# A replanned order of steps for a fused sigmoid-attention and token-mixing kernel on one core

## The chip, the cores and the metric

The kernel runs on one core of one Trainium2 chip. A core has five engines that run their own instruction queues side by side: TensorE (PE, matrix products and transposes into PSUM banks; PEld is its weight load), VectorE (DVE), ScalarE (ACT), GpSimd (POOL) and SyncE (SP, which here issues most DMAs). The metric is the device time of one execution in microseconds (us), lower is better. The runs before the change took 180.97, 180.97 and 181.77 us, a median of 180.97.

## The reference

For 8 batches, 12 heads, 448 rows and a head size of 64, in float32:

```python
scores = scale * np.matmul(q, k.transpose(0, 1, 3, 2)) - np.log(S)
attn = 1.0 / (1.0 + np.exp(-scores))
x = attn @ v                      # heads side by side: (8, 448, 768)
W_tok = scale * np.einsum('bsd,btd->bst', x @ w_q, x @ w_k)
mixed = np.einsum('bst,btd->bsd', W_tok, x)
out = np.maximum(mixed, 0.0) @ w_out
```

A sigmoid replaces the softmax, so no row sums are needed. The kernel never forms `W_tok`: it multiplies `(x w_k)^T x` first (a 64 x 768 matrix per batch), then mixes with `x w_q`.

## The kernel before

**Units of work.** The 96 head-batches go in 24 quads of four heads: quad n is heads 4j to 4j+3 of batch u, n = 3u + j. A quad's 448 rows are cut into 7 blocks of 64. For each quad there are these steps; the letters are those of the order string `PLAN`, which is written out in full and read by one loop at the end:

- Loads (SP queue, L177 and L188) bring q, k and v of a quad in float32 into one of eight buffers of 448 KB. `ORDER` is the order of loads and casts.
- Casts to bf16: most on POOL (L201 and L224 for q and k, L218 for v, 128 x 896 each). A `.` ahead of a name in `ORDER` puts that cast on VectorE, a capital letter on ScalarE, and a `*` drops both load and cast and issues one casting DMA from POOL's queue straight into the bf16 buffer (L213).
- Transposing q and k, in one of three forms. Form `c` with `d`: POOL swaps 32-row blocks with six copies (L163, L166, L169, two each, function `arrange`), then VectorE makes two stream transposes of 128 x 448 (L285); `c` needs the copies of L166 and `d` those of L169. Form `r` with `s` and `z`: no POOL copies, but VectorE makes two transposes of 128 x 448 (L278) and four of 32 x 448 (L254). Form `q` with `k` (and `a` with `b`): TensorE transposes, VectorE copies the result out (L316, L302).
- `S`, 168 times: TensorE makes one block's scores for four heads (L328, four matmuls of 64 x 448) into two banks, ScalarE applies the sigmoid (L333, 128 x 896).
- `P` (also `p`, `R`), 168 times: TensorE accumulates attention times v (L350); after the seventh block VectorE casts the result `xt` out (L359).
- `x`, `X`: TensorE transposes `xt` (L388, L372), VectorE copies `xn` (L401, L377). `W`, `w`, `L`, `l`: x times w_q and w_k (L425, L413); at the end of a tiled pass one half is copied (`wpart`, L420) and VectorE adds the other half (L421). `N`, `U`, `T`, `M`: the small products of the mixing (L440, L454, L469, L493, L507), the relu at L480 or L478.
- `O`, `o`, `Q` (also `I`, `i`): a part of the output product (L539, L579, L620); after the last part VectorE or ScalarE copies `o` out (L550, L552, L584, L653; the letter says which engine) and a DMA stores it.

**What sets the order.** Every engine takes its instructions strictly in the order in which the loop records them; there is no scheduler. Eight PSUM banks are handed out by the list `BANKS`, one entry per step that needs one. A cast is recorded on POOL as soon as its load is recorded and its target is free: the bf16 buffer `qk16` exists twice, so the q and k casts of quad n come after the transposes of quad n-2; `v16` exists four times.

Of the kernel before, what the change touches and what calls it, by code (L numbers as in the profile page):

```python
# [932 lines left out]
```

## Time and profile before

| | before |
|---|---|
| time, median of three runs | 180.97 us (180.97 to 181.77) |
| span of the profiled execution | 180.1 us |
| TensorE busy | 169.6 us, 94% |
| ScalarE busy | 159.0 us, 88% |
| VectorE busy | 145.6 us, 81% |
| GpSimd busy | 121.4 us, 67% |
| bytes moved by DMA | 47.31 MB |

The page gives the span of the profiled execution, from its first to its last instruction; its own time is not listed apart from the three runs. The 0.87 us between span and median lie outside the instructions.

How to read it: a busy share is a mean over stages. GpSimd's 67%, for example, hides that it does almost nothing in the last fifth of the span. In a timeline row the first number is the start in us from the span's start, the second the length, then engine, line, operation, output and input with their shapes, and in brackets what the engine sat idle for just before. TensorE rows overlap in their ends, so its pace is read from starts.

### The profile page before, as it was taken

The numbers are of one execution on the slowest core, as the hardware profiler recorded it, in microseconds if no ns is written. First come the engines' busy times: TensorE is split into PE (matmuls) and PEld (weight loads), VectorE is DVE, ScalarE is ACT, GpSimd is POOL, SyncE is SP. The second block draws the span as 40 slices with busy tenths as digits, with TensorE's granted clock in tenths as the row PEclk, the third lists the DMA queues.
The fourth block names the chain that finished last, engine by engine and source line by source line (L and its number), as shares of the span: only waits on it lengthen the run. The fifth ranks groups of instructions, "written<-read, shape, count | busy, mean of one in ns | idle before, by whom it ended". The sixth has DMA issues, their size and how long they took to land.

```text
span 180.1 us, 7907 instructions
## 1 busy us (share of the span) xinstructions
PE 169.6 (94%) x3440; PEld 112.2 (62%) x3440; DVE 145.6 (81%) x227; ACT 159.0 (88%) x208; POOL 121.4 (67%) x166
## 2 busy tenths in 40 slices
PE   7698899889899999999999999999999999999990
PEld 3334445444575555445667786678887788888660
DVE  3578899997989896889999999979898886768351
ACT  4699999999899999999999999999999989976300
POOL 1028799689999999999999999979979910010000
PEclk9999999999999999999999999999999999999999
DMA  5999999999999998899998889987795523505876
GB/s 177 355 372 349 322 383 381 280 302 356 342 294 349 339 265 267 217 319 365 343 300 315 217 288 305 342 322 213 200 338 173 135 64 73 137 4 122 201 208 175
DMA packets 27475, 47.31 MB, mean 263 GB/s; under 512 B 3888, under 2 KB 23600, under 8 KB 27440
## 3 DMA queue, kind: packets, MB, share of 16 engines
q1 hardware_dynamic: 26160, 44.64, 78.0%
q0 software_dynamic: 800, 1.18, 3.6%
q10 hardware_dynamic: 480, 0.98, 1.5%
q8 instruction: 27, 0.44, 1.0%
q14 instruction: 8, 0.07, 0.1%
HBM read 35.78 MB, written 11.01 MB: 260 GB/s over the span
## 4 chain that ended last, share of the span: by engine, by line
PE 56%; POOL 16%; DMA 15%; DVE 5%; ACT 2%; issue 2%; SPq 1%; POOLq 0%
PE banks L539 15%; PE banks L350 10%; PE banks L328 10%; PE banks L620 8%; DMA q<-in_q_dram 6%; POOL qk L201 5%; DMA w<-in_moe_w_k_dram 4%; DMA k<-in_k_dram 3%; POOL qk L169 3%; DMA wout<-wout 2%; ACT at L333 2%; POOL v L218 2%; PE banks L579 2%; PE banks L413 2%; POOL swap L163 2%
## 5 line engine op out<-in xcount | busy, mean ns | idle before, releaser
L333 ACT ACTIVATE at<-banks 128x896 bf16<-128x896 f32 x168 | 140.0, 948 | 3.4 <-PE banks L328 3.0
L328 PE MATMUL banks<-qk 64*64 64x448 bf16 x672 | 62.2, 358 | 3.3 <-ACT at L333 1.6
L350 PE MATMUL banks<-at,v 64*64 64x448 bf16 x672 | 47.3, 351 | 0.8 <-ACT at L333 0.7
L328 PEld LDWEIGHTS <-qk 64*64 64x64 bf16 x672 | 25.9, 105 | 20.7 <-issue 13.2
L539 PE MATMUL banks<-wout,mx 64*64 64x384 bf16 x672 | 36.6, 323 | 0.0
L201 POOL CAST qk<-k 128x896 bf16<-128x896 f32 x19 | 22.8, 1199 | 10.6 <-DVE qk L302 9.7
L350 PEld LDWEIGHTS <-v 64*64 64x64 bf16 x672 | 23.2, 107 | 8.6 <-issue 1.7
L539 PEld LDWEIGHTS <-mx 64*64 64x64 bf16 x672 | 23.3, 107 | 4.5 <-issue 0.5
L359 DVE CAST xt<-banks 128x896 bf16<-128x896 f32 x22 | 23.8, 1083 | 2.3 <-PE banks L350 1.8
L620 PE MATMUL banks<-wout,mx 128*128 128x384 bf16 (+1 forms) x138 | 24.4, 320 | 0.0
L480 DVE TENSOR_SCALAR mx<-banks 128x1024 bf16<-128x1024 f32 (+3 forms) x22 | 21.3, 972 | 1.9 <-PE banks L493 0.7
L201 POOL CAST qk<-q 128x896 bf16<-128x896 f32 x17 | 20.4, 1198 | 2.6 <-DMA q<-in_q_dram 1.3
L218 POOL CAST v<-v 128x896 bf16<-128x896 f32 x22 | 20.6, 950 | 1.4 <-DMA v<-in_v_dram 0.4
L620 PEld LDWEIGHTS <-mx 128*128 128x128 bf16 x138 | 12.3, 98 | 9.8 <-issue 3.2
L285 DVE STREAM_TRANSPOSE qk<-qk 128x448 f32<-128x448 f32 x28 | 17.0, 627 | 0.4 <-POOL qk L166 0.3
L163 POOL COPY swap<-qk 32x448 uint32<-32x448 uint32 x28 | 15.5, 554 | 2.3 <-DVE qk L201 0.7
L166 POOL COPY qk<-qk 32x448 uint32<-32x448 uint32 x28 | 15.8, 566 | 1.6
L169 POOL COPY qk<-swap 32x448 uint32<-32x448 uint32 x28 | 15.8, 564 | 1.6
L254 DVE STREAM_TRANSPOSE qk<-qk 32x448 f32<-32x448 f32 x24 | 15.3, 636 | 0.6
L422 POOL COPY wq<-wqk 64x448 bf16<-64x448 bf16 x3 | 1.7, 555 | 15.7 <-DVE wqk L421 15.7
L653 DVE COPY o<-banks 128x384 f32<-128x384 f32 x12 | 6.6, 553 | 5.7 <-PE banks L620 5.3
L653 ACT COPY o<-banks 128x384 f32<-128x384 f32 x9 | 4.4, 490 | 7.1 <-PE banks L620 6.9
(91 smaller groups left out, 206.5 us busy)
## 6 DMA issues: line engine op xcount, KB each, us to landing
q<-in_q_dram SPq DMA_DIRECT2D x24, 448.0 KB, 6.6
v<-in_v_dram SPq DMA_DIRECT2D x24, 448.0 KB, 6.3
k<-in_k_dram SPq DMA_DIRECT2D x23, 448.0 KB, 7.0
out_dram<-o SPq DMA_DIRECT2D x50, 192.0 KB, 3.9
wout<-in_moe_w_out_dram POOLq DMA_DIRECT2D x2, 576.0 KB, 12.2
wout<-wout SPq DMA_DIRECT2D x12, 96.0 KB, 6.2
out_dram<-o ACTq DMA_DIRECT2D x4, 192.0 KB, 3.5
k<-in_k_dram SPq DMA_DIRECT2D x1, 256.0 KB, 5.6
```

The lines of the kernel that those rows point to most:

```text
L163: eng.tensor_copy(out=z[lo], in_=w[hi, 0])
L169: eng.tensor_copy(out=w[lo, 1], in_=z[lo])
L201: COPY[e](out=f[:, :, "qk".index(nm)].rearrange("p e i d y -> p e y i d"), in_=ld.pop((nm, n)),)
L218: COPY[e](out=t16.rearrange("p b i d -> p (b i d)"), in_=ld.pop((nm, n)).rearrange("p b x -> p (b x)"),)
L285: nc.vector.transpose(out=qk[n][:, t].rearrange("p t i n -> p (t i n)").bitcast(F32), in_=w)
L328: nc.tensor.matmul(sc[HALF[h], g, 0:S], qk[n][HALF[g], h, 1, i, :], qk[n][HALF[g], h, 0].rearrange("p i n -> p (i n)"), start=True, stop=True,
L333: inst = nc.scalar.activation(at, sc[:, :, 0:S], ACTF.Sigmoid, bias=attn_bias, scale=attn_scale)
L350: nc.tensor.matmul(ps[HALF[g], h, 0:S], ld["v16", n][HALF[h], g, i, :], ats[n, i][HALF[h], g, :], start=(i == 0), stop=(i == NI - 1),)
L359: read(fb, COPY[eng](out=xt(u, j)[:, :, 0:S], in_=ps[:, :, 0:S]))
L480: inst = nc.vector.tensor_scalar(dst, ps, moe_scale, 0.0, ALU.mult, ALU.max)
L539: nc.tensor.matmul(ps[HALF[x], y, 0:NB], mx[HALF[y], u, b, 64 * (i - 3 * y) : 64 * (i - 3 * y) + 64], wout16[HALF[y], slot(y, b), x * NB : ...
L620: nc.tensor.matmul(ps, mxs[w][:, 2 * S * c + m * P : 2 * S * c + (m + 1) * P], wout16[:, c, w0:w1], start=(c == 0), stop=(c == NC - 1),)
```

## The change

The change replaces the tables that set the order and the way buffers are given out. What is computed is the same.

- `PLAN` and `BANKS` are written anew as one table: each step carries its bank. 168 `S`, 168 `P`-type and the other product steps remain in number, with some exceptions: six filler matmuls `F` and four fillers `f` at the start are gone, one `X` became an `x`, one `U` a `T` and one quad less is transposed on TensorE. In the changed program TensorE changes 59 times between whole and quartered use of its array once it has started.
- The transposing forms of quads 0 to 23 were `aarqrrqcrccccrccccrccccc` and are `aarrrrqcrccccrcccccccccc`: quad 3 goes from TensorE (`q`) to VectorE (`r`), and quad 18 from VectorE alone (`r`) to POOL copies with VectorE (`c`).
- Casts: q1, k1, q2, q12, q22, k22 and v22 were on VectorE and v19 on ScalarE. Now only k2 is on VectorE, and v6 and v23 come by casting DMAs; all others are on POOL.
- Output copies: ScalarE makes fewer of them before the last sigmoid, VectorE more.
- Tile pools become fixed buffers used in turn; a load takes any free one of the eight load buffers.

```diff
     PLAN = (
-        "ffSSSffKSSF11aSb1SFFrSFSFSSFSqSPPsPPSPzkPSPSPPPSxSrSsPPPPSPPS"
...
+        "S67 S23 K01 S67 S45 S23 a01 S45 b S67 1 S23 S45 S23 P01 S67 p p S23 r R S45 s p P S67 z "
...
     ORDER = (
-        ".q1 .k1 k2 .q2 q3 v0 w2 k3 v1 k4 q4 v2 w0 k5 q5 w1 v3 W5 v4 q6 k6 w4 k7 v5 q7 v6 q8 k8 k9 "
-        "q9 v7 q10 v8 k10 v9 k11 q11 k12 k13 v10 .q12 q13 v11 v12 v13 q14 k14 k15 q15 v14 q16 k16 "
-        "v15 q17 k17 k18 q18 q19 v16 v17 v18 k19 V19 W3 q20 .q22 q21 k20 W6 k21 .k22 v20 q23 k23 "
-        "v21 .v22 v23 "
+        "q1 k1 q2 .k2 v0 v1 q3 w2 k3 q4 k4 W5 v2 w0 v3 k5 q5 v4 w1 W3 q6 v5 k6 W6 q7 w4 *v6 k7 k8 "
+        "q8 q9 k9 v7 k10 v8 q10 v9 q11 k11 v10 k12 q12 k13 v11 q13 k14 v12 v13 q14 k15 q15 v14 "
+        "q16 k16 k17 q17 v15 v16 v17 q18 k18 v18 k19 q19 v19 k20 q20 q21 v20 k21 q22 k22 v21 v22 "
+        "k23 *v23 q23 "
...
+    lds = [singles.tile([P, 2 * RUN + PAD], F32, name=f"ld{n}") for n in range(8)]
+    v16s = [singles.tile([P, 2, NI, HD], BF16, name=f"v16{n}") for n in range(4)]
+    qks = [singles.tile([P, 2, 2, NI, NP], BF16, name=f"qk{n}") for n in range(8)]
+    qk16s = [singles.tile([P, 2, 2, NI, 32, 2], BF16, name=f"qk16{n}") for n in range(2)]
...
+    def turn(nm, bufs):
+        turns[nm] = turns.get(nm, -1) + 1
+        return bufs[turns[nm] % len(bufs)]
+
+    def borrow(key):
+        held[key] = free.pop(0)
+        return held[key]
...
-                pq[n] = p_c16.tile([P, 2, 2, NI, 32, 2], BF16, tag="qk16", name="qk16")
+                pq[n] = turn("qk16", qk16s)
...
-            if len(ring) >= 8 and ring[-8] not in cast:
+            if not free:
                 break
...
+        if (nm, n) in held:
+            free.append(held.pop((nm, n)))
         pump_loads()
```

The tables show where steps went only in the instruction order. Three places matter here. In these rows the changed program's lines stand about twelve higher: its L213 is L201 of before, L230 is L218, L175, L178 and L181 are L163, L166 and L169, L297 is L285, L371 is L359, L432 and L433 are L420 and L421. `ld` is a load buffer, `qk16` the cast q and k, `v16` the cast v, `swap` a scratch tile; numbers behind a name tell buffers apart.

POOL, the last quads. Before, from the k cast of quad 21 (its q was cast earlier) to the casts of v21 and v23; quad 22's casts are on VectorE, so only its copies stand here:

```order
L201 CAST qk16_2870<-k32_2619 128x2x2x224
L163 COPY swap_2881<-qk16_2870 32x448 x2
L166 COPY qk16_2870<-qk16_2870 32x448 x2
L169 COPY qk16_2870<-swap_2881 32x448 x2
L422 COPY wq21_120<-wqk1_118 64x448
L218 CAST v16_3060<-v32_2782 128x896
L163 COPY swap_3280<-qk16_3207 32x448 x2
...
L201 CAST qk16_3433<-q32_3056 128x2x2x224
L201 CAST qk16_3433<-k32_3058 128x2x2x224
L163 COPY swap_3436<-qk16_3433 32x448 x2
...
L218 CAST v16_3443<-v32_3209 128x896
L218 CAST v16_3624<-v32_3235 128x896
```

The same piece of POOL's order in the changed program, from quad 22's casts to quad 23's last copy:

```order
L213 CAST qk161_121<-ld1_101 128x2x2x224
L213 CAST qk161_121<-ld2_102 128x2x2x224
L175 COPY swap_3010<-qk161_121 32x448 x2
...
L230 CAST v161_109<-ld3_103 128x896
L230 CAST v162_110<-ld4_104 128x896
L213 CAST qk160_120<-ld6_106 128x2x2x224
L225 DMA v163_111<-in_v_dram 128x2x448
L213 CAST qk160_120<-ld7_107 128x2x2x224
L175 COPY swap_3235<-qk160_120 32x448 x2
L178 COPY qk160_120<-qk160_120 32x448 x2
L181 COPY qk160_120<-swap_3235 32x448 x2
```

Quad 22's two casts came to POOL, v21 and v22 now stand ahead of quad 23's casts and copies instead of behind them, and the casting DMA of v23 stands between quad 23's two casts.

VectorE, quad 7's two transposes (`qk16_781` before, `qk7` from `qk160` in the changed program), before:

```order
L285 STREAM_TRANSPOSE qk_977<-qk16_781 128x448
L401 COPY xn_950<-banks_88 128x2x4x128
L285 STREAM_TRANSPOSE qk_977<-qk16_781 128x448
L359 CAST xt5_116<-banks_88 128x2x448
L278 STREAM_TRANSPOSE qk_1086<-qk16_923 128x448 x2
```

And now:

```order
L413 COPY xn1_127<-banks_67 128x2x4x128
L371 CAST xt5_95<-banks_67 128x2x448
L297 STREAM_TRANSPOSE qk7_119<-qk160_120 128x448 x2
L290 STREAM_TRANSPOSE qk0_112<-qk161_121 128x448 x2
L442 CAST wqk1_97<-banks_67 128x448
```

Both transposes moved behind the cast of `xt5`; the q and k casts of quad 9, which reuse the buffer, wait for them on POOL.

VectorE, the start of quad 23's transposes, before:

```order
L552 COPY o_3727<-banks_88 128x768
L285 STREAM_TRANSPOSE qk_3756<-qk16_3433 128x448
L420 COPY wpart_3767<-banks_88 128x448
L421 TENSOR_TENSOR wqk0_117<-banks_88,wpart_3767 128x448
L359 CAST xt3_114<-banks_88 128x2x448
L285 STREAM_TRANSPOSE qk_3756<-qk16_3433 128x448
```

And now:

```order
L564 COPY o2_132<-banks_67 128x768
L297 STREAM_TRANSPOSE qk7_119<-qk160_120 128x448
L432 COPY wpart_3571<-banks_67 128x448
L433 TENSOR_TENSOR wqk0_96<-banks_67,wpart_3571 128x448
L371 CAST xt3_93<-banks_67 128x2x448
L297 STREAM_TRANSPOSE qk7_119<-qk160_120 128x448
```

This piece stands as it stood: nothing moved among these six. The next output part on TensorE (L539 before) writes the banks that the copy and the addition read.

More of the change, by code (lines that the diff above doesn't have):

```diff
@@ L67 @@
     banks16 = banks.rearrange("p b x -> p (b x)").bitcast(BF16).rearrange("p (b x) -> p b x", b=8)
-    BANKS = (
[11 rows of a table removed]
-    )
-    BANKS = BANKS.split()[::-1]
+    bank = []
     readers = [([], []) for _ in range(8)]
@@ L90, in bank2 @@
     def bank2():
-        lo, hi = (int(b) for b in BANKS.pop())
+        lo, hi = (int(b) for b in bank.pop())
         take(lo, hi)
@@ L96, in bank1 @@
     def bank1():
-        b = int(BANKS.pop())
+        b = int(bank.pop())
         take(b)
@@ L119, with halves @@
     wq2s = [singles.tile([P, S], BF16, name=f"wq2{n}") for n in range(2)]
+    lds = [singles.tile([P, 2 * RUN + PAD], F32, name=f"ld{n}") for n in range(8)]
+    v16s = [singles.tile([P, 2, NI, HD], BF16, name=f"v16{n}") for n in range(4)]
+    qks = [singles.tile([P, 2, 2, NI, NP], BF16, name=f"qk{n}") for n in range(8)]
+    qk16s = [singles.tile([P, 2, 2, NI, 32, 2], BF16, name=f"qk16{n}") for n in range(2)]
+    t16s = {nm: [singles.tile([P, NI, 2, HD], BF16, name=f"{nm}16{n}") for n in range(2)] for nm in "qk"}
+    xn_bufs = [singles.tile([P, 4, D], BF16, name=f"xn{n}") for n in range(2)]
+    mx_bufs = [singles.tile([P, 2 * 12 * 256], BF16, name=f"mx{n}") for n in range(2)]
+    o_bufs = [singles.tile([P, 2 * NB], F32, name=f"o{n}") for n in range(3)]
+    turns = {}
+    free = list(lds)
+    held = {}
+    def turn(nm, bufs):
[4 more added lines that the diff above has]
+        return held[key]
+    def halves(t):
+        return t[:, 0 : 2 * RUN].rearrange("p (g x) -> p g x", g=2)
     ctx.enter_context(tc.manual_schedule())
@@ L186, in load1 @@
             return
-        t = p_ld.tile([P, 2, NI * HD], F32, tag="ld", name=nm + "32")
+        t = halves(borrow((nm, n)))
         eng.dma_start(
@@ L675 @@
     KA, KB = slice(0, 3), slice(3, 7)
-    q0 = p_ld.tile([P, 2, NI * HD], F32, tag="ld", name="q32")
-    k0 = p_ld.tile([P, 2, NI * HD], F32, tag="ld", name="k32")
+    q0 = halves(borrow(("q", 0)))
+    k0 = halves(borrow(("k", 0)))
     src = {
@@ L791, in cast_next @@
         pump()
-    q016 = p_c16.tile([P, NI, 2, HD], BF16, tag="q16", name="q16")
-    k016 = p_c16.tile([P, NI, 2, HD], BF16, tag="k16", name="k16")
+    q016 = turn("q", t16s["q"])
+    k016 = turn("k", t16s["k"])
     def cast_part(t16, t32, r, e):
@@ L805, with tr_part @@
     cast |= {("q", 0), ("k", 0)}
+    free.append(held.pop(("q", 0)))
     pump_loads()
-    qk[0] = p_qk.tile([P, 2, 2, NI, NP], BF16, tag="qk", name="qk")
-    def tr_part(nm, t16, r, e):
+    qk[0] = qks[0]
+    def tr_part(nm, t16, r, e, b=None):
+        if b:
+            bank.append(b)
         fb, _, ps = bank2()
@@ L815, in tr_part @@
         ))
-    tr_part("q", q016, IA, "v")
-    tr_part("q", q016, IB, "s")
-    tr_part("k", k016, KA, "v")
+    tr_part("q", q016, IA, "v", "01")
+    tr_part("q", q016, IB, "s", "23")
+    tr_part("k", k016, KA, "v", "45")
     cast_part(k016, k0, KB, "v")
+    free.append(held.pop(("k", 0)))
+    pump_loads()
     used |= {("q", 0), ("k", 0)}
@@ L826 @@
     quads_r = []
-    for t in PLAN:
+    for t, b in PLAN:
+        assert not bank
+        if b:
+            bank.append(b)
         if t == "F":
@@ L903 @@
                 pump()
-    assert not chunks and not opened and not BANKS
+    assert not chunks and not opened and not bank
 _INS = ['q', 'k', 'v', 'moe_w_q', 'moe_w_k', 'moe_w_out']
```

48 lines of the change are left out of this document (16 added, 32 removed), and 31 rows, old and new, of tables (BANKS, PLAN).

## The prediction

> **What bounds the kernel now.** I read the page first, then busy time by stretches, the chain of waits near its end, and last GpSimd's own instructions. The page's busy line and GpSimd's row of its 40 slices:
>
> ```profile
> PE 169.6 (94%) x3440; PEld 112.2 (62%) x3440; DVE 145.6 (81%) x227; ACT 159.0 (88%) x208; POOL 121.4 (67%) x166
> POOL 1028799689999999999999999979979910010000
> ```
>
> GpSimd's 67% is a mean over two regimes: from the fourth slice to the 32nd (13 to 144 us; a slice is 4.5 us) it is nearly always busy, afterwards it has almost nothing to do. Busy time in stretches (columns: us, then PE, PEld, DVE, ACT, POOL with instruction counts, clock, DMA share, GB/s):
>
> ```profile
> 6.00:42.00 36.00, 31.30 (x622) 16.75 (x622) 30.76 (x45) 35.37 (x44) 25.53 (x31) 1.00 1.06 344
> 42.00:62.00 20.00, 19.49 (x345) 11.44 (x344) 17.35 (x28) 19.39 (x24) 18.73 (x25) 1.00 1.02 339
> 62.00:155.00 93.00, 92.90 (x2026) 66.21 (x2025) 81.28 (x116) 90.77 (x116) 75.88 (x105) 1.00 0.81 252
> ```
>
> Up to 42 us ScalarE is the full engine (35.4 of 36.0) and TensorE idles 4.7 us. From 62 to 155 us TensorE is full (92.9 of 93.0). The chain of waits says the same of the end:
>
> ```profile
> 147.21 0.98 PE banks L539 x24
> ...
> 166.03 9.88 PE banks L620 x66
> ...
> 175.94 0.36 DVE o L642
> ```
>
> So from the output part at 147.21 on, the rest is TensorE's own fixed work and the last stores: whatever delays that part delays the end by as much, and nothing behind it gives the time back.
>
> GpSimd is the engine that the change loads. Between the first cast of quad 9 and the last copy of quad 23 it does this (groups by operation; busy us, mean ns, idle before):
>
> ```profile
> L201 POOL CAST qk<-k 128x896 bf16<-128x896 f32 x14 | 16.8, 1199 | 0.6 <-DMA k<-in_k_dram 0.3
> L201 POOL CAST qk<-q 128x896 bf16<-128x896 f32 x13 | 15.6, 1201 | 1.3 <-DVE qk L285 1.0
> L166 POOL COPY qk<-qk 32x448 uint32<-32x448 uint32 x26 | 14.7, 566 | 1.5
> L169 POOL COPY qk<-swap 32x448 uint32<-32x448 uint32 x26 | 14.7, 565 | 1.5
> L163 POOL COPY swap<-qk 32x448 uint32<-32x448 uint32 x26 | 14.4, 554 | 2.2 <-DVE qk L201 0.7
> L218 POOL CAST v<-v 128x896 bf16<-128x896 f32 x14 | 12.8, 931 | 0.4
> L434 POOL COPY wq<-wqk 64x448 bf16<-64x448 bf16 x4 | 2.2, 554 | 0.3
> L422 POOL COPY wq<-wqk 64x448 bf16<-64x448 bf16 x1 | 0.6, 553 | 0.1
> ```
>
> Its paces, and the two ends of that stretch, from its timeline:
>
> ```profile
> 44.76 1.21 POOL L201 CAST qk<-k 128x896 bf16<-128x896 f32 x1 [0.30 <-DMA k<-in_k_dram]
> ...
> 90.99 0.55 POOL L434 COPY wq<-wqk 64x448 bf16<-64x448 bf16 x1
> 91.61 1.20 POOL L201 CAST qk<-q 128x896 bf16<-128x896 f32 x1
> ...
> 97.67 0.93 POOL L218 CAST v<-v 128x896 bf16<-128x896 f32 x1
> 98.54 1.19 POOL L201 CAST qk<-q 128x896 bf16<-128x896 f32 x1
> ...
> 118.45 1.21 POOL L201 CAST qk<-q 128x896 bf16<-128x896 f32 x1 [0.98 <-DVE qk L285]
> ...
> 131.99 1.17 POOL L163 COPY swap<-qk 32x448 uint32<-32x448 uint32 x2 [0.66 <-DVE qk L201]
> ...
> 139.26 1.17 POOL L166 COPY qk<-qk 32x448 uint32<-32x448 uint32 x2
> 140.48 1.16 POOL L169 COPY qk<-swap 32x448 uint32<-32x448 uint32 x2
> ```
>
> A `c` quad (two casts, six copies) takes 97.67 - 91.61 = 6.06 us, a v cast about 0.90 (98.54 - 97.67 = 0.87, a little more ahead of a copy), the `wq` copy 91.61 - 90.99 = 0.62. As a check on these prices: thirteen quads, one cast more, thirteen v casts (the fourteenth only starts at the edge), five `wq` copies make 78.8 + 1.2 + 11.7 + 3.1 = 94.8, and the two waits 1.64: 96.4, against 141.64 - 44.76 = 96.9 measured.
>
> How late GpSimd may be is read on VectorE, which needs quad 23's copies:
>
> ```profile
> 41.81 0.63 DVE L285 STREAM_TRANSPOSE qk<-qk 128x448 f32<-128x448 f32 x1
> 42.37 1.05 DVE L359 CAST xt<-banks 128x896 bf16<-128x896 f32 x1
> ...
> 144.99 0.63 DVE L285 STREAM_TRANSPOSE qk<-qk 128x448 f32<-128x448 f32 x1
> 145.55 0.62 DVE L420 COPY wpart<-banks 128x448 f32<-128x448 f32 x1
> 146.27 0.62 DVE L421 TENSOR_TENSOR wqk<-banks,wpart 128x448 bf16<-128x448 f32 x1
> ```
>
> The L166 copies for quad 23 ended at 139.26 + 1.17 = 140.43, the transpose that needs them began at 144.99: 4.56 us to spare.
>
> **The change, part by part.** *GpSimd.* In the same stretch, from quad 9's first cast to quad 23's last copy, the changed order holds fourteen `c` quads (quad 18 is new), two casts for quad 13, sixteen v casts (v19, v21, v22 are new here), four `wq` copies and the issue of one casting DMA. The issue is priced by the same kind of instruction:
>
> ```profile
> L670 POOL DMA_DIRECT2D wout<-in_moe_w_out_dram x2 | 1.7, 836 | 0.0
> ```
>
> Sum: 14 x 6.06 + 2 x 1.2 + 16 x 0.90 + 4 x 0.62 + 0.84 = 84.8 + 2.4 + 14.4 + 2.5 + 0.8 = 104.9 us, without any wait. That is 8.0 more than the 96.9 of before.
>
> *When the stretch starts.* Quad 9's casts wait for quad 7's transposes, which now stand behind the cast of `xt5`. If that cast ends where it did (42.37 + 1.05 = 43.42), two transposes end at 44.6, and the start is 44.6. The upper bound comes from VectorE's first 35 us, where quad 3 now needs six stream transposes for one copy:
>
> ```profile
> 14.06 2.64 DVE L254 STREAM_TRANSPOSE qk<-qk 32x448 f32<-32x448 f32 x4
> 17.47 1.09 DVE L316 COPY qk<-banks 128x1792 bf16<-128x1792 bf16 x1 [0.77 <-PE banks L238]
> 18.48 1.08 DVE L359 CAST xt<-banks 128x896 bf16<-128x896 f32 x1
> 20.12 0.69 DVE L401 COPY xn<-banks 128x1024 bf16<-128x1024 bf16 x1 [0.56 <-PE banks L388]
> ```
>
> Four of 32 rows take 2.64, the two of 128 rows about 1.2 by L285's 0.63, less 1.09 for the copy: 2.8 us more; the tiled `T` in place of `U` adds one copy of about 0.56. The idle 0.77 and 0.56 can take up 1.3 of that. A slip of 2.0 us puts the start at 46.6. I take 45.0: later rows up to the `xt5` cast have idle that can absorb more, and the lower end rests on a row directly.
>
> *The end.* Quad 23's L166 copies end 1.2 us before the stretch does: 45.0 + 104.9 - 1.2 = 148.7. VectorE then makes the transpose, the `wpart` copy and the addition; in the trace that is 146.27 + 0.62 - 144.99 = 1.9 us, and TensorE's output part at 147.21 waits for the banks that they read. It starts no sooner than 148.7 + 1.9 = 150.6, which is 3.4 later than 147.21. The L169 copies and the second transpose come late by about as much, so they add nothing. 180.1 + 3.4 = 183.5 of span; with the 0.87 between span and median, **184.4**.
>
> *VectorE's casts* (four in that stretch, v22 among them) are gone: worth nothing here, since TensorE, then GpSimd, is what VectorE serves. The wait of 0.66 in the rows above, GpSimd on a VectorE cast, goes with them; my sum holds no wait.
>
> *ScalarE.* Before the last sigmoid it loses the v19 cast, three copies of 128 x 384, one of 128 x 768 and one of two output halves, and gains one relu and one copy of 448 columns:
>
> ```profile
> L653 ACT COPY o<-banks 128x384 f32<-128x384 f32 x9 | 4.4, 490 | 7.1 <-PE banks L620 6.9 <-ACT at L333 0.2
> ```
>
> Four such copies are 2.0 us; with the cast (0.93 if it is as long as GpSimd's) and the larger copy (twice the columns, under 1.0) it is at most 3.9. What it gains I bound by two such copies, 1.0, and take 3 as the net. TensorE's full stretch hides this: 0. Without that cover it would be worth up to 3.
>
> *TensorE.* The fillers, 56 small transposes of quad 3 and some tiling forms go; all but a few tenths lies before 42 us, where TensorE had 4.7 us idle: 0. The array changes its tiling 68 times before and 60 times now in the program, but from quad 3 on 55 times in both, so the saving lies in that same idle stretch: 0. Fixed buffers and bank numbers add no instruction: 0; what they cost as waits is in the stretches above.
>
> *The casting loads.* v6 is issued just ahead of quad 7's last cast and must be there for quad 6's first L350. Loads and issue:
>
> ```profile
> 36.33 1.20 POOL L201 CAST qk<-q 128x896 bf16<-128x896 f32 x1 [1.29 <-DMA q<-in_q_dram]
> v<-in_v_dram SPq DMA_DIRECT2D x24, 448.0 KB, 6.3
> wout<-in_moe_w_out_dram POOLq DMA_DIRECT2D x2, 576.0 KB, 12.2
> 48.45 0.38 PE L350 MATMUL banks<-at,v 64*64 64x448 bf16 x2
> ```
>
> Issued at about 36.3 less 0.84 and landing after 6.3 to 12.2 us it is there at 41.8 to 47.7, before 48.45: 0. [...]
>
> **Rivals.** *1. GpSimd's lateness is covered.* If the start is early, VectorE's queue has run ahead, and TensorE finds other work while the transpose waits, the end moves by less than 0.9: about 181.3. For it: 4.56 us were spare, and GpSimd is idle for over 30 us at the end. Against: VectorE and TensorE take their work in order, and the sum eats the 4.56.
>
> *2. Faster.* The place is 42 to 62 us, where TensorE and ScalarE take turns as the limit. TensorE had 19.5 of 20.0 busy there, but ScalarE's 3 us less and fewer waits might let the full stretch start up to 2 us sooner, if GpSimd kept up: 179.0. It decides if quad 23's copies end before 145, that is, if GpSimd's stretch takes less than 101 us. Against: fourteen times 6.06 alone is 84.8.
>
> *3. Slower still.* GpSimd's stretch begins late, at 46.6, because VectorE's early slip is not absorbed, and it waits twice on VectorE as it did before (1.64): 3.4 + 1.6 + 1.6 = 6.6 later, 187.6.
>
> *4. The v6 load is late.* If it took twice 12.2, it would land at 59.9, 11.4 after 48.45; the lateness of GpSimd would vanish in it: about 192. Nothing in the rows calls for that.
>
> **How the numbers follow.** Forecast (182.5 to 186.2) 0.60, rival 1 (180.1 to 182.5) 0.20, rival 2 0.15, rivals 3 and 4 together 0.05. A measurement of this kernel tells about 0.5%, 0.9 us, from no change: faster means below 180.1, slower above 181.9. Rival 1's upper quarter lies above 181.9, so slower is 0.60 + 0.05 + 0.05 = 0.70, the same 0.15, faster 0.15. The forecast's own range has its lower end from a start at 44.6 and a first transpose not held up fully, its upper end from a start at 46.6 with some wait. For 8 in 10 it reaches down through most of rival 1: 180.6 to 186.4.
>
> **What would show it.** Right: GpSimd busy until about 150, quad 23's last copy near 149.9 and not 141.6; VectorE waiting for L166's copies by several us in the last five quads; TensorE with idle gaps after 105, where it had none; the piece from the late output part to the end still about 33 us. The start is right if quad 9's first cast waits for a VectorE transpose and begins at 44.6 to 46.6. Wrong: a `c` quad that takes clearly less than 6.06, the first transpose of quad 23 without a wait, or TensorE still full from 62 to 155.

## The result

The changed kernel takes **188.22 us** (median of 4 runs, 187.23 to 189.36) against 181.37 for the kernel before beside it: a ratio of 1.0344, 95% interval 1.0264 to 1.0425, so 3.4% slower. The forecast was slower, 184.4, with a range up to 186.4: the sign was right, the size was not, and the experiments show that most of the reason was not right either. The profiled execution took 188.91 us, its span 187.1.

The page of the changed kernel (busy line, three of its rows of 40 slices of 4.7 us, the chain of waits by engine, and two groups with their idle time before and what ended it):

```profile
PE 170.8 (91%) x3400; PEld 112.7 (60%) x3400; DVE 143.6 (77%) x227; ACT 159.1 (85%) x205; POOL 130.3 (70%) x178
...
DVE  3357999996998898798999867678758786786431
...
POOL 1167899991699999999999999999999970010000
PEclk9756999999999999999999999999999999999999
...
PE 56%; DVE 17%; POOL 16%; DMA 5%; issue 2%; ACT 1%; SPq 0%; POOLq 0%; DVEq 0%
...
L345 ACT ACTIVATE at<-banks 128x896 bf16<-128x896 f32 x168 | 141.4, 927 | 9.2 <-PE banks L340 8.2
...
L213 POOL CAST qk<-ld 128x896 bf16<-128x896 f32 x41 | 47.9, 1199 | 6.8 <-DVE qk L297 5.8
```

GpSimd (POOL) is full from the twelfth slice to the 32nd, as forecast. But three things stand here that the forecast did not have: VectorE is full from the fifth slice to the ninth and its share of the chain went from 5% to 17%, while GpSimd's stayed at 16%; TensorE's clock falls to half between the second and the fourth slice (0.50 granted from 7.18 to 17.42 us); and ScalarE's sigmoids wait 8.2 us for scores (3.0 in the kernel before).

The forecast's own landmarks: VectorE's timeline around quad 7, then GpSimd's two ends, then VectorE's transpose that needs quad 23's copies, and TensorE's one wait for the addition that follows it:

```profile
44.48 0.69 DVE L413 COPY xn<-banks 128x1024 bf16<-128x1024 bf16 x1 [0.68 <-PE banks L400]
46.19 1.09 DVE L371 CAST xt<-banks 128x896 bf16<-128x896 f32 x1 [1.02 <-PE banks L362]
47.32 1.17 DVE L297 STREAM_TRANSPOSE qk<-qk 128x448 f32<-128x448 f32 x2
```

```profile
48.55 2.31 POOL L213 CAST qk<-ld 128x896 bf16<-128x896 f32 x2 [5.79 <-DVE qk L297]
...
150.80 1.17 POOL L178 COPY qk<-qk 32x448 uint32<-32x448 uint32 x2
152.03 1.17 POOL L181 COPY qk<-swap 32x448 uint32<-32x448 uint32 x2
```

```profile
152.00 0.65 DVE L297 STREAM_TRANSPOSE qk<-qk 128x448 f32<-128x448 f32 x1 [0.65 <-POOL qk L178]
```

```profile
PE banks L551 <- DVE wqk L433: 0.2, 1, 0.2
```

GpSimd's stretch is 153.20 - 48.55 = 104.65 us long; the forecast's sum was 104.9. It begins at 48.55 and not at 45.0, because the xt5 cast, ahead of quad 7's transposes, ends at 47.3 instead of 43.4. Put 48.55 into the forecast's sum and the span comes to 187.0, against 187.1 measured. So on paper everything closes, with one term mis-sized. But look at the waits at that place: VectorE idles only 0.65 us for the copies, and TensorE only 0.2 us for the addition, although the output part starts at 153.94, 6.7 us later than in the kernel before. A GpSimd that is in time at this place alone would have moved it by about 0.2 us: TensorE was late already. The experiments show where it lost the time.

**A finer ruler.** Whole times of one kernel scatter by about 1%, too much for terms of 1 us. The first sigmoids of quads 2, 5, 9, 13, 18 and 23 cut each profiled execution into stretches, and those of one order agree to 0.1 us where nothing touches them (quads 13 to 18 took 32.94 or 32.95 us in seven kernels). Busy time in these stretches, of the changed kernel (columns: us, then PE, PEld, DVE, ACT, POOL, clock, DMA share, GB/s):

```profile
19.19:38.42 19.23, 15.56 (x270) 8.09 (x268) 18.69 (x30) 17.66 (x22) 18.01 (x23) 1.00 1.07 348
38.42:62.41 23.99, 22.52 (x469) 12.25 (x465) 21.15 (x32) 23.34 (x29) 17.11 (x24) 1.00 0.92 266
...
120.40:156.94 36.54, 35.24 (x934) 28.59 (x930) 27.15 (x40) 32.50 (x41) 31.32 (x45) 1.00 0.70 197
```

and of the kernel before's order in the changed kernel's code (the experiment on the buffers, below), an execution with little waiting for loads:

```profile
17.46:34.59 17.13, 15.69 (x270) 8.31 (x266) 16.03 (x24) 17.13 (x22) 15.71 (x19) 1.00 1.09 344
34.59:57.46 22.87, 21.91 (x464) 13.03 (x464) 21.22 (x32) 22.87 (x29) 21.00 (x29) 1.00 1.06 331
...
114.21:148.36 34.15, 34.15 (x930) 28.00 (x926) 29.70 (x42) 33.21 (x42) 25.00 (x36) 1.00 0.70 206
```

In the latter ScalarE has no idle moment from quad 2 to 9 and TensorE none from quad 9 to 23. Between these two executions lie 8.75 us, 4.95 of them ahead of quad 9's first sigmoid. All kernels of this study, us per stretch:

| kernel | to quad 2 | 2-5 | 5-9 | 9-13 | 13-18 | 18-23 | to the end | span |
|---|---|---|---|---|---|---|---|---|
| before | 17.95 | 17.12 | 23.46 | 25.08 | 32.19 | 34.25 | 30.04 | 180.1 |
| before's order, fixed buffers (e12) | 17.46 | 17.13 | 22.87 | 24.59 | 32.16 | 34.15 | 30.03 | 178.4 |
| changed | 19.19 | 19.23 | 23.98 | 25.05 | 32.94 | 36.54 | 30.20 | 187.1 |
| + fillers (e1) | 18.29 | 18.62 | 24.20 | 24.96 | 32.94 | 36.29 | 30.06 | 185.4 |
| quad 7 early (e3) | 18.33 | 18.67 | 23.41 | 24.96 | 32.95 | 35.24 | 30.07 | 183.6 |
| five casts back (e4) | 18.54 | 18.68 | 23.70 | 25.31 | 32.94 | 36.59 | 30.04 | 185.8 |
| fillers, quad 3 back (e5) | 18.36 | 18.57 | 23.01 | 24.98 | 33.38 | 35.87 | 30.10 | 184.3 |
| fillers, quad 18 back (e6) | 18.45 | 18.64 | 24.23 | 24.95 | 34.62 | 34.23 | 30.18 | 185.3 |
| quads 3, 7, 18 and four casts back (e7) | 18.36 | 18.57 | 23.10 | 25.91 | 34.62 | 35.62 | 30.11 | 186.3 |
| fillers, no GpSimd copies (e11) | 18.37 | 18.63 | 24.06 | 24.95 | 32.95 | 35.42 | 30.06 | 184.5 |
| before's head, changed rest (e9) | 17.56 | 17.13 | 22.90 | 24.95 | 32.95 | 36.28 | 30.06 | 181.8 |
| the same, no GpSimd copies (e14) | 17.65 | 17.10 | 23.02 | 24.96 | 32.95 | 34.82 | 30.22 | 180.7 |
| changed head, before's rest (e10) | 18.34 | 18.68 | 23.63 | 24.59 | 32.40 | 35.87 | 30.03 | 183.5 |
| before + GpSimd's load (e8) | 17.45 | 17.15 | 22.86 | 28.65 | 33.89 | 33.98 | 30.04 | 184.0 |
| before without fillers (e2) | 20.10 | 17.13 | 22.86 | 24.59 | 32.17 | 34.24 | 30.04 | 181.1 |
| e12, v19 by a casting load (e13) | 18.57 | 17.05 | 22.86 | 24.59 | 32.16 | 34.87 | 30.17 | 180.3 |

### The profile page after: what moved, and what is told of

Read it like the earlier page. It is cut to its first block, busy times and chain, and to the rows that moved or that the text cites. A ratio compares the mean times of both kernels' runs of the same rounds, so it can differ in the third digit from the quotient of the medians.

```text
span 187.1 us, 7829 instructions
## 1 busy us (share of the span) xinstructions
PE 170.8 (91%) x3400; PEld 112.7 (60%) x3400; DVE 143.6 (77%) x227; ACT 159.1 (85%) x205; POOL 130.3 (70%) x178
## 4 chain that ended last, share of the span: by engine, by line
PE 56%; DVE 17%; POOL 16%; DMA 5%; issue 2%; ACT 1%; SPq 0%; POOLq 0%; DVEq 0%
PE banks L340 12%; PE banks L362 10%; PE banks L551 10%; PE banks L632 10%; POOL qk L213 6%; DVE qk L266 4%; DVE xt L371 3%; DMA ld<-in_k_dram 3%; POOL swap L175 3%; PE banks L591 3%; DVE qk L290 2%; POOL qk L178 2%; POOL qk L181 2%; PE banks L437 2%; DMA ld<-in_q_dram 2%; POOL v L230 2%
## 5 line engine op out<-in xcount | busy, mean ns | idle before, releaser
L340 PE MATMUL banks<-qk 64*64 64x448 bf16 x672 | 66.5, 371 | 5.4 <-DVE xt L371 1.5
L213 POOL CAST qk<-ld 128x896 bf16<-128x896 f32 x41 | 47.9, 1199 | 6.8 <-DVE qk L297 5.8
L362 PE MATMUL banks<-at,v 64*64 64x448 bf16 x672 | 50.6, 356 | 1.8 <-issue 0.6
L340 PEld LDWEIGHTS <-qk 64*64 64x64 bf16 x672 | 26.9, 107 | 25.7 <-issue 17.4
L371 DVE CAST xt<-banks 128x896 bf16<-128x896 f32 x22 | 23.9, 1084 | 5.2 <-PE banks L362 4.8
L230 POOL CAST v<-ld 128x896 bf16<-128x896 f32 x22 | 20.3, 934 | 2.6 <-DMA ld<-in_v_dram 2.0
L297 DVE STREAM_TRANSPOSE qk<-qk 128x448 f32<-128x448 f32 x30 | 18.7, 633 | 4.0 <-POOL qk L178 3.2
L175 POOL COPY swap<-qk 32x448 uint32<-32x448 uint32 x30 | 16.7, 556 | 1.8
L178 POOL COPY qk<-qk 32x448 uint32<-32x448 uint32 x30 | 16.7, 556 | 1.8
L181 POOL COPY qk<-swap 32x448 uint32<-32x448 uint32 x30 | 16.6, 555 | 1.8
L564 DVE COPY o<-banks 128x768 f32<-128x768 f32 x11 | 10.5, 953 | 2.7 <-ACT at L345 1.4
L665 DVE COPY o<-banks 128x384 f32<-128x384 f32 x14 | 7.8, 555 | 4.6 <-PE banks L632 4.0
L413 DVE COPY xn<-banks 128x1024 bf16<-128x1024 bf16 (+1 forms) x15 | 9.4, 629 | 2.3 <-PE banks L400 2.2
```

The costliest lines, as they stand in the source:

```text
L175: eng.tensor_copy(out=z[lo], in_=w[hi, 0])
L178: eng.tensor_copy(out=w[hi, 0], in_=w[lo, 1])
L213: COPY[e](out=f[:, :, "qk".index(nm)].rearrange("p e i d y -> p e y i d"), in_=ld.pop((nm, n)),)
L230: COPY[e](out=t16.rearrange("p b i d -> p (b i d)"), in_=ld.pop((nm, n)).rearrange("p b x -> p (b x)"),)
L340: nc.tensor.matmul(sc[HALF[h], g, 0:S], qk[n][HALF[g], h, 1, i, :], qk[n][HALF[g], h, 0].rearrange("p i n -> p (i n)"), start=True, stop=True,
L362: nc.tensor.matmul(ps[HALF[g], h, 0:S], ld["v16", n][HALF[h], g, i, :], ats[n, i][HALF[h], g, :], start=(i == 0), stop=(i == NI - 1),)
```

## The experiments

Ratios are to the kernel before, run beside them, with 95% intervals. Where the edited kernel has one line more, its line numbers are one higher than the changed kernel's.

### The fillers

Added to the changed kernel (e1, 16 matmuls by the code and the trace), and taken out of the kernel before with their banks (e2, 14 matmuls); the expectations count 20. The diff is e1's:

```diff
-"S67 S23 K01 S67 S45 S23 a01 S45 b S67 1 S23 S45 S23 P01 S67 p p ...
+"f7 f7 S67 S23 f5 f5 K01 S67 F5 S45 F3 S23 a01 F5 S45 b F7 F7 S67 1 F3 S23 F5 S45 F3 S23 P01 S67 p p ...
```

> The changed kernel with the 20 filler matmuls put back at the places in the first steps where the kernel before had them (the first seven between the loads' first transposes and quad 4); nothing else differs. Theory A (the fillers kept TensorE's clock up): in the changed kernel the granted clock is 0.5 from 7.2 to 17.4 us after the start; with the fillers that stretch is gone or shorter than 4 us, quad 2's first sigmoid comes at 18.0 instead of 19.2, quad 5's at 36.5 to 37.5 instead of 38.4, quad 9's first GpSimd cast starts at 47.0 instead of 48.5, and the end is 1.0 to 2.0 us earlier than the changed kernel's, so 186 to 187. Theory B (the fillers only filled gaps; the lateness comes from VectorE's and TensorE's own added work): the clock may change, but quad 9's first cast still starts at 48.5 and the end moves by less than 0.5 us.

> The kernel before without its 20 filler matmuls, order and banks of everything else untouched. Theory A (fillers hold the clock): a half-rate stretch of about 10 us appears near 7 us after the start, quads 2 to 5 begin their sigmoids about 1 us later than before, and since quad 23's GpSimd copies had 4.6 us to spare but TensorE was full from 62 us on, the end is 0.5 to 1.5 us later: 181.5 to 182.5. Theory B (the idle time of TensorE in the first 42 us absorbs it): clock full as before, or half with no consequence, time within 0.4 us of before.

Measured: e1 1.0337 (1.0258 to 1.0417), e2 1.0019 (0.9974 to 1.0064). Busy time from 7 to 17.4 us, in the changed kernel:

```profile
7.00:17.40 10.40, 8.60 (x94) 4.57 (x98) 6.42 (x11) 9.09 (x12) 6.21 (x7) 0.51 1.04 401
```

with the fillers again:

```profile
7.00:17.40 10.40, 8.32 (x100) 3.80 (x98) 6.54 (x11) 10.07 (x13) 7.38 (x8) 1.00 1.04 400
```

and in the kernel before without them, a little later:

```profile
10.50:14.00 3.50, 3.30 (x33) 1.60 (x32) 2.69 (x6) 2.53 (x4) 1.36 (x2) 0.50 0.99 348
14.00:17.50 3.50, 2.84 (x52) 1.34 (x48) 3.13 (x6) 3.50 (x6) 2.90 (x4) 0.50 0.96 350
```

The mechanism of theory A is there both ways: without fillers the granted clock is half for 10.24 us in both profiled executions (7.18 to 17.42 us in the changed kernel, 9.30 to 19.54 in e2), and early sigmoids come later (quad 2: 0.9 us in the changed kernel, over 2 in the one before). Quad 9's first cast starts 1.3 us earlier with fillers, and the span is 1.8 shorter. But the half-rate stretch is not of one length from run to run (mean clocks of 0.970 to 0.982 for the changed kernel, 1.0 with fillers), and neither ratio shows a difference that can be told. By its time e2 is theory B's case (0.3 us from the kernel before). So: up to 1.8 us in an execution, about 0.5% or less in the time.

No long pause of TensorE stands at the fall: in the changed kernel its longest gap up to 17.42 us is 1.45 us (6.31 to 7.76), and the clock fell all the same.

What differs is how busy TensorE was just before. From 3.77 us, where the trace's record of the clock begins, at full rate, to the fall at 7.18 us, so for 3.41 us, it was busy for 1.75 us in the changed kernel, and for 2.89 in the same piece with the fillers. In the five executions that lost the clock in their first 12 us, TensorE was busy for 48 to 62% of as long a piece ahead of the loss; the kernel before kept it behind such a piece with 57% (6.1 to 9.5 us), so no sharp limit can be read off. Fillers make the loss rarer, not impossible: of the eleven profiled executions that have them one lost the clock there (e13, for 3.4 us), of the five without them four did (the changed kernel and e2 for 10.2 us, e4 and e10 for 3.4 us; e3 not).

### Quad 7's transposes back ahead of the cast

```diff
-S23 M45 S67 P01 p P S23 R x45 R S67 R P c S23 d W5 w ...
+S23 M45 c d S67 P01 p P S23 R x45 R S67 R P S23 W5 w ...
```

> The changed kernel with quad 7's two transposes moved back ahead of the cast of xt5 (two tokens of the order, moved by two places); nothing else differs. Theory A (GpSimd's stretch is the bound and begins when quad 7's second transpose ends): quad 9's first cast starts at 44.5 to 46 instead of 48.5, GpSimd's stretch keeps its 104.7 us, quad 23's last copies end 2.5 to 4 us earlier and so does the kernel: 184 to 185.5. Theory B (VectorE and TensorE are late by themselves in the first 45 us, and the later part is bound by TensorE): quad 9's cast is earlier but the end moves by less than 0.7 us.

Measured: 1.0264 (1.0177 to 1.0352). Its profiled execution had next to no half-rate clock, so it stands beside e1: 0.8 us less from quad 5 to 9, 1.05 less from 18 to 23, and 1.7 less of span. This is theory A's direction at about half its size: GpSimd starts 3.6 us earlier than in e1 (quad 9's copies L178 end at 48.4 instead of 52.0), and 1.7 of it reach the end.

### Casts off GpSimd

Four casts back on VectorE, v19 on ScalarE:

```diff
- ... k12 q12 k13 ... q19 v19 k20 ... q22 k22 v21 v22
+ ... k12 .q12 k13 ... q19 V19 k20 ... .q22 .k22 v21 .v22      (and in PLAN four tokens 1 and one 2, at which VectorE and ScalarE make them)
```

> The changed kernel with four of the casts it gave to GpSimd (q12, q22, k22, v22) on VectorE again and one (v19) on ScalarE again, placed where the kernel before had them in the order; nothing else differs. Theory A (GpSimd is the bound): its stretch from quad 9's first cast to quad 23's last copy is 4 x 1.2 less, so about 100 instead of 104.7 us, and the end is 3 to 4.5 us earlier: 183.5 to 185. Theory B (TensorE with the new order and tiling is the bound, GpSimd only follows it): GpSimd shows waits in place of the work taken off, quad 23's copies end as late as before, and the end moves by less than 0.7 us.

Measured: 1.0284 (1.0205 to 1.0363), span 185.8. GpSimd was relieved as meant (its stretch is 101.1 us instead of 104.65), quad 23's copies end 3.7 us before VectorE wants them, and the end did not move against e1: theory B. Part of it is an accident of the edit. The v19 cast delays a sigmoid at the one place where TensorE cannot do without it. ScalarE's timeline, then TensorE's:

```profile
124.65 0.93 ACT L230 CAST v<-ld 128x896 bf16<-128x896 f32 x1
125.48 0.92 ACT L345 ACTIVATE at<-banks 128x896 bf16<-128x896 f32 x1
```

```profile
126.82 0.72 PE L362 MATMUL banks<-at,v 64*64 64x448 bf16 x9 [1.27 <-issue]
```

That the value matmuls wait for this sigmoid is my reading, since the profile names no releaser.

### Quad 3, quad 18, and all of it together

Each of these has the fillers. Quad 3 by TensorE (e5) and quad 18 by VectorE (e6):

```diff
-P S45 r R23 s p S01 S67 z R R S45 p R S01 P S67 r R45 ...
+P S45 q01 R23 k p S67 S45 R R S01 p R S45 P S67 r R45 ...
```

```diff
-R23 c S67 d R p R P S01 o45 P S67 o P S01 Q S67 O x23 ...
+R23 r S67 R p R P S01 o45 P s S67 o P S01 Q z S67 O x23 ...
```

> The changed kernel with fillers (as in the first experiment) and with quad 3 again laid out by TensorE transposes and one VectorE copy, in place of VectorE's six stream transposes. Theory A (VectorE's first 38 us are the early loss): from quad 2's first sigmoid to quad 5's took 17.0 us in the kernel before and 18.6 with fillers alone, VectorE being busy 18.1 of 18.6; with quad 3 back it takes 16.8 to 17.3, quad 9's first sigmoid comes 1.5 to 2 us earlier (59.3 instead of 61.1), and the end is 1 to 2 us earlier than with fillers alone (profiled span 183.5 to 184.5 instead of 185.4). Theory B (the lateness is made up or made anew later, by GpSimd): early sigmoids come earlier but the end moves by less than 0.5 us. Theory C (the early loss comes from TensorE's own order, quad 2's transposes standing five score groups later): the stretch keeps its 18.6 us.

> The changed kernel with fillers and with quad 18 laid out again on VectorE (six stream transposes) in place of GpSimd's six copies; GpSimd keeps all the casts. Theory A (GpSimd's lateness reaches TensorE through VectorE's queue, most of it at quad 19's first transpose, which waited 2.2 us): GpSimd's stretch is 3.7 us shorter, that wait is under 0.3 us, from quad 18's first sigmoid to quad 23's takes 34.5 to 35 us instead of 36.3, and the end is 1.3 to 2 us earlier (profiled span 183.4 to 184.1 instead of 185.4). Theory B (TensorE's new order and banks set this stretch by themselves): the wait goes, the stretch stays at 36 us or more, and the end moves by less than 0.5 us.

> The changed kernel with all of: fillers, quad 3 laid out by TensorE again, quad 7's transposes ahead of the xt5 cast, and q12, q22, k22 and v22 cast on VectorE again. Quad 18 is laid out by VectorE too. Theory A (three places, clock, VectorE's start and GpSimd's tail, make up the whole loss): the sums add, 1.7 + 1.7 + 1.7 plus up to 1 from quad 7, so a profiled span of 179 to 181, the time of the kernel before. Theory B (the new order and bank plan cost something of their own, which none of these edits touch): it stays 2 us or more above the kernel before, span 182 or more.

Measured: e5 1.0283 (1.0247 to 1.032), e6 1.0359 (1.0299 to 1.0418), e7 1.0405 (1.0368 to 1.0441).

*Quad 3:* quads 2 to 5 keep their 18.6 us, against theory A, although VectorE has 2.2 us less to do there (15.9 busy). Its timeline says why:

```profile
16.90 1.09 DVE L372 CAST xt<-banks 128x896 bf16<-128x896 f32 x1 [0.66 <-PE banks L363]
18.93 1.09 DVE L329 COPY qk<-banks 128x1792 bf16<-128x1792 bf16 x1 [0.94 <-PE banks L251]
21.70 1.09 DVE L372 CAST xt<-banks 128x896 bf16<-128x896 f32 x1 [1.67 <-PE banks L363]
22.82 1.17 DVE L291 STREAM_TRANSPOSE qk<-qk 128x448 f32<-128x448 f32 x2
```

The copy waits 0.94 for quad 3's transposes on TensorE (the second cast for them, on GpSimd, only ends at 17.64), the next xt cast 1.67 for value matmuls, and quad 4's transposes begin at 22.82 as in e1: what VectorE saved, it now waits for TensorE. The edit undoes the kind of layout, not the order around it: nearest to theory C. So VectorE's load alone is not what costs 1.5 us there; that TensorE's order does is what is left, and no run tests it by itself. The span of 184.3 lies in theory A's range for another reason: 1.2 us are saved from quad 5 to 9.

*Quad 18:* GpSimd's stretch is shorter and VectorE waits for it nowhere from quad 17 on; the span stays (185.3 against 185.4):

```profile
86.27:120.89 34.62, 32.31 (x668) 22.94 (x664) 30.56 (x43) 31.47 (x41) 32.68 (x44) 1.00 0.87 278
120.89:155.12 34.23, 34.23 (x934) 28.28 (x930) 27.26 (x40) 32.28 (x40) 25.92 (x38) 1.00 0.71 198
```

Quads 18 to 23 take 34.2 as before, but quads 13 to 18 pay 1.7 for VectorE's four small transposes: neither theory. *All of it (e7):* worse than e1, theory B, with quads 9 to 13 and 13 to 18 longer by 1.0 and 1.7 us. My reading is that VectorE has no room in the changed order for the work that was taken from it: what the edits take off GpSimd's queue they put into VectorE's.

### GpSimd's load in the kernel before

```diff
-... SONOScTSOSOSOOdSPOSrOSPPPGPPSPPPSPPsPSPOSPOSOzSQSXPc ...
+... SONOScTSOSOSOOdSPOSOSPPPGPPSPPPSPPcPSPOSdPOSOSQSXPc ...      (and q12, q22, k22, v22, v19 without their marks)
```

> The kernel before with GpSimd's added load alone: quad 18's layout moved from VectorE to GpSimd (its first transpose now stands where the small transposes stood) and the casts q12, q22, k22, v22 (VectorE) and v19 (ScalarE) moved to GpSimd; order, fillers and banks stay. The prediction's sum: 8.0 us more on GpSimd less the 4.56 us that quad 23's copies had to spare, so 3.4 us later, 184 to 185. Theory A (GpSimd's lateness costs what VectorE's waits for it pass on to TensorE, about 2 us in the changed kernel): 1.5 to 2.5 us later, with VectorE waits on GpSimd at quads 18 or 19. Theory B (covered, the first rival of the prediction): less than 0.9 us later.

Measured: 1.027 (1.0226 to 1.0315), 4.9 us, more than either theory and more than the prediction's sum. The place is neither quad 23 nor 18 but the first cast that was moved, quad 12's, where there is hardly any room. VectorE's timeline and TensorE's waits there:

```profile
70.53 0.68 DVE L377 COPY xn<-banks 128x1024 bf16<-128x1024 bf16 x1
73.04 0.65 DVE L285 STREAM_TRANSPOSE qk<-qk 128x448 f32<-128x448 f32 x1 [1.83 <-POOL qk L166]
74.26 0.65 DVE L285 STREAM_TRANSPOSE qk<-qk 128x448 f32<-128x448 f32 x1 [0.57 <-POOL qk L169]
74.83 0.52 DVE L653 COPY o<-banks 128x384 f32<-128x384 f32 x1
```

```profile
PE banks L350 <- DVE o L653: 2.0, 1, 2.0
```

```profile
ACT at L333 <- PE banks L328: 4.1, 4, 2.3
```

VectorE waits 2.4 us for GpSimd with an output copy behind it; TensorE waits 2.0 us for the banks that this copy reads; ScalarE then waits 4.1 for scores, and quads 9 to 13 take 28.65 instead of 24.59. Quads 13 to 18 pay another 1.7. Part of the 4.1 us is the clock's: TensorE, busy for only 2.11 of the 4.13 us up to 76.13, runs at half rate from there to 79.54. One of the four executions kept its clock and took 185.36 us, 0.4 less than the median. The prediction's mechanism (a transpose that waits for GpSimd holds up TensorE through VectorE's queue) exists and costs more than its own length. In the changed order it does not do so at quad 12, whose copies come just in time.

### Which half of the order

Up to the 42nd score group (the 42nd `S`, the last of quad 5) both orders have done the same work, so they can be joined there.

```diff
 e9:   order, casts and banks of the kernel before | to here, then the changed kernel's
 e10:  order, casts and banks of the changed kernel | to here, then the kernel before's
```

> The order of the kernel before up to its 42nd score group (quads 0 to 5, with fillers, its casts and its banks), then the changed kernel's order from there on, all in the changed kernel's fixed buffers. At that place both orders have done the same work. What each theory expects, by the stretches between first sigmoids: before took 17.95 to quad 2, 17.1 from quad 2 to 5, 23.5 to 9, 25.1 to 13, 32.2 to 18, 34.25 to 23, 30.05 to the end; the changed kernel 19.2, 19.2, 24.0, 25.05, 32.9, 36.5, 30.2. Theory A (the loss lies half in the first 42 groups, by the clock and by VectorE's queue, and half after, by waits for GpSimd and by order): quad 5 at 35, quads 13 to 18 still 32.9, quads 18 to 23 between 35 and 36.5, span 182 to 183. Theory B (all of it is GpSimd's late part, the early lateness would be made up): the span stays at 185 or more. Theory C (all lies in the early part): 180 to 181.

> The other half: the changed kernel's order up to its 42nd score group (no fillers, quad 3 on VectorE, its casts), then the order of the kernel before, with its casts on VectorE and ScalarE and quad 18 on VectorE, in the changed kernel's fixed buffers. Theory A: quad 5 at 38 to 38.5, then 23 to 23.5, 25.1, 32.2, 34.25 and 30.05 as before, so a span of 183 to 184: early lateness is carried to the end in full, since ScalarE and TensorE have no idle time from there on to make it up. Theory B (the early lateness would be made up): 181 or less. Theory C (all lies in the early part): 185 or more.

Measured: e9 1.0113 (1.0067 to 1.0159), e10 1.024 (1.0126 to 1.0354); the two add to 3.5%, the whole change being 3.4%. So **more than half of the loss is made in the first 42 score groups** (to about 44 us), the rest later: theory A, with more weight on the head. By the ratios it is two thirds, but e10's interval is wide; by the table, 4.95 of 8.75 us lie ahead of quad 9. e10's rest runs at the kernel before's pace up to quad 18, without making up anything. From 18 to 23 it took 1.7 more than that, 1.16 of it one wait of TensorE for which the profile names no cause; that stays open.

### What GpSimd's lateness is worth

```diff
-        if KIND[n] in "er":
+        if KIND[n] in "cer":        (no copies; e11: in the changed kernel with fillers; e14: in e9 with quad 7 early)
```

> The changed kernel with fillers, without the six GpSimd copies of each of the fourteen quads that it lays out so (3.7 us per quad; VectorE then transposes what is not laid out, so the scores of those quads are other numbers, at the same cost on every other engine). Nothing moves to another engine, so this is the worth of GpSimd's lateness alone. Theory A (part of the loss is waits for GpSimd): ScalarE's idle time between the first sigmoids of quads 18 and 23 falls from 3.8 to under 2 us, that stretch from 36.3 to 34.3, and the span from 185.4 to 182.5 to 183.5. Theory B (GpSimd's lateness is the whole late loss, as the prediction had it): 180 to 181.5. Theory C (order and banks alone set the late part): over 184.8.

> The kernel before's order for the first 42 score groups, the changed kernel's from there, with quad 7's two transposes ahead of the xt5 cast, and without GpSimd's six copies for each of the fourteen quads (whose scores are other numbers then). Neither the early lateness nor GpSimd can hold anything up here, so what is left above the kernel before is the changed order from quad 7 on, by itself. Theory A (order alone costs 0.4 from quad 9 to 13, 0.75 from 13 to 18 and 1 to 1.2 from 18 to 23): those stretches take 24.9, 32.9 and 35.2 to 35.4 us, span 180.5 to 181. Theory B (the late loss needs GpSimd or the early lateness): 24.6, 32.2 and 34.3, span 178.4 to 179.

Measured: e11 1.0231 (1.0096 to 1.0366), e14 1.0109 (1.0066 to 1.0153). Fifteen quads of form `c` lose their copies, quad 7 among them (the expectations say fourteen). In e11 GpSimd is idle for half of quads 13 to 18 and more of 18 to 23 (16.91 busy of 32.95 us, 12.69 of 35.42), and still e11 is only 0.9 us of span ahead of e1: between theories A and C. Quad 19's first transpose in the changed kernel, VectorE's timeline:

```profile
119.83 0.68 DVE L413 COPY xn<-banks 128x1024 bf16<-128x1024 bf16 x1
122.83 0.65 DVE L297 STREAM_TRANSPOSE qk<-qk 128x448 f32<-128x448 f32 x1 [2.32 <-POOL qk L178]
123.40 1.05 DVE L371 CAST xt<-banks 128x896 bf16<-128x896 f32 x1
```

and the same place without GpSimd's copies:

```profile
119.00 0.63 DVE L297 STREAM_TRANSPOSE qk<-qk 128x448 f32<-128x448 f32 x1
120.78 1.09 DVE L371 CAST xt<-banks 128x896 bf16<-128x896 f32 x1 [1.15 <-PE banks L362]
```

The wait of 2.3 us for GpSimd is replaced by one of 1.15 us for TensorE: the next instruction in VectorE's order could not have started much earlier. In e14 neither GpSimd nor the head can hold anything up, and quads 9 to 23 still take 1.8 us more than in e12 (0.37, 0.79 and 0.67): theory A. ScalarE's waits there between 17 and 152 us:

```profile
ACT at L346 <- PE banks L341: 2.6, 9, 0.6
ACT wq L445 <- DVE wqk L443: 0.8, 1, 0.8
ACT mx L491 <- PE banks L506: 0.7, 1, 0.7
```

That is the late order by itself, with its banks and its other split of copies and casts between the engines: many small waits, one of 0.8 us of ScalarE on VectorE's `wqk` cast, which stands in every kernel with the changed order. Between e9 and e14 quads 18 to 23 differ by 1.46 us; the ratios of the two do not tell them apart. So GpSimd's late part is worth 0.9 to 1.5 us in the profiled executions.

### The buffers alone

```diff
 e12:  PLAN, banks and ORDER of the kernel before, in the changed kernel's code
```

> The changed kernel's code with fixed buffers given out in turn, but with the kernel before's order of steps, of casts and of banks: the buffers alone. Every theory so far expects the time of the kernel before, within 0.5%, since no engine gains or loses an instruction and the transfers have the same eight buffers. If the loads come in another order (a buffer is now free again when its cast has read it, not when the eighth load after it is due), the first 20 us could be up to 1 us longer or shorter.

Measured: 0.9963 (0.9915 to 1.0012), stretches as in the kernel before to 0.1 us where no load is waited for: the fixed buffers cost nothing.

### Which engine sets the pace

```diff
- ... v18 k19 V19 W3 q20 .q22 q21 k20 W6 k21 ...
+ ... v18 k19 *v19 q20 .q22 q21 k20 k21 ...      (W3, W6 and an earlier W5 record no instruction)
```

> The kernel before's order in the fixed buffers (as in the run of the buffers alone), with one change: v19, which ScalarE cast between sigmoids (0.93 us), comes by a casting load that GpSimd issues (0.8 us), so ScalarE has one operation less between quads 18 and 23. Theory A (ScalarE's row of sigmoids, idle for only 1.9 us between quads 2 and 23, sets the pace of the kernel before): the stretch from quad 18 to quad 23 falls from 34.2 to 33.3 us and the time by 0.5%. Theory B (TensorE sets it): ScalarE waits for scores instead, the stretch and the time stay.

Measured: 1.0005 (0.9969 to 1.004); quads 18 to 23:

```profile
115.23:150.09 34.86, 34.62 (x930) 28.04 (x926) 29.01 (x42) 32.62 (x41) 25.84 (x37) 1.00 0.67 194
```

ScalarE has less to do (32.62 against 33.21) and waits more; the stretch does not shrink, it took 0.7 us more here, for which I have no cause. So ScalarE does not set the pace: theory B. That TensorE does is what is left; it is full (34.62 of 34.86 busy, and 34.15 of 34.15 in e12), with ScalarE less than 1 us behind it, but no run took work off it.

## Why the prediction was wrong

- **"GpSimd becomes the bound"**: its stretch was right (104.9 forecast, 104.65 measured, without one wait in it), its part in the time was not. With its copies left out the changed kernel gets back about 1 us (e11); with five casts or quad 18's copies moved from it to VectorE and ScalarE the end stays (e4, e6): those engines pay for what GpSimd saves. The other engines need nearly as long for the same piece by themselves: from quad 9's to quad 23's first sigmoid 93.3 us without GpSimd's copies (e11), 94.2 with them (e1). That the sum closed at 187.0 with the measured start was luck.
- **"When the stretch starts": 45.0, measured 48.55. This is the term that failed in the sum**, and what stands behind it is the step that failed in the reasoning: that the early lateness would be absorbed, so that GpSimd's 3.4 us alone reach the end. The bound from below, "if that cast ends where it did", held the xt5 cast at 43.42; it ended at 47.28. I had taken VectorE's lateness as something that its own idle time would absorb (a slip of at most 2.0), and what TensorE loses as covered by its 4.7 us of idle time. Instead the first 42 groups lose 3.4 us against the profiled execution of the kernel before (3.9 against e12's), and nothing makes them up (e10): ScalarE is nearly full from quad 5 to 9 (23.34 of 23.99 us in the changed kernel), TensorE from 9 to 13 (24.89 of 25.05). Where the head loses, to quad 9 and against e12: the clock up to 1.5 us (e1), then to quad 2 0.8, quads 2 to 5 1.5, quads 5 to 9 about 1.1. The cause of the last three stays open: in quads 2 to 5 VectorE is busy for 18.1 of 18.6 us in e1 and quad 4's transposes begin at 22.9 instead of 20.8, but e5 took 2.2 us off VectorE there and gained nothing.
- **"The fillers ... go: 0"** was wrong in kind. They held TensorE's clock up in most executions (in ten of the eleven profiled ones that have them it did not fall in the first 12 us), in the very stretch in which I priced TensorE's work by its idle time at full clock.
- **Order of TensorE, banks: 0.** Wrong by 1.8 us (e14 against e12), in small waits that no sum over instructions shows. With the head's 4.95 and up to 1.5 for GpSimd this makes 8.2 of the 8.75 us; the rest is not placed.
- **Buffers: 0**, right (e12). **ScalarE's 3 us hidden**, right: its other operations between quads 2 and 23 came down from 9.5 to 6.4 us, and e13 shows for the kernel before that such a gain buys nothing while TensorE is full.
- **The end**: from quad 23 on it takes the same time in all kernels (30.0 to 30.2), as forecast. "The 0.87 between span and median" is no constant: in every execution on record time and span differ by 1.7 to 1.9 us, and 0.87 sets the span of one execution against the median of others. The forecast's 3.4 us do not hang on it. **The v6 load** (fourth rival) took 13.4 us, landing at about 48.2, beyond my 47.7; quad 6 was itself later by 3.4 us, and TensorE's list has no wait for it. No run shows a load that takes twice 12.2 us, as that rival assumes: the casting loads took 13.4 (v6) and 4.7 (v23) in the changed kernel and 7.2 (v19) in e13.
- **Rivals**: the first one, GpSimd's lateness covered but for 0.9 us, was the better description of that engine, and the third one, VectorE's early slip not absorbed, of the head; its 187.6 came nearest, though not by its two waits of GpSimd. Neither had the clock or the late order in it.
- **"What would show it"**: most signs of being right came true. GpSimd was busy to 153.20, VectorE waited 3.2 us for L178's copies from quad 19 on, TensorE got idle gaps, and from the late output part to the end it took 33.2 us. They could not tell a GpSimd that sets the time from one that costs 1 us of it; the length of the waits at quad 23 could.

## What to carry to other kernels

When two or three engines are all nearly full and take their work in order, a reordering is not priced by adding up the load of the engine that gets more: cut the run at marks that both versions share, and find the stretch that grew. An engine that is busy without a gap need not set the time: ask who waits for it and how long, then leave its work out and see whether the end moves. Price of matmuls that compute nothing: look at the granted clock before calling them free.
